# First slot of a fused attention and expert kernel: transposes into another PSUM pool, and a new order of the last routing, the tables and the splits

## The chip, the cores and the metric

The kernel runs on one core of a Trainium2 chip. The metric is device time in microseconds (us) of one launch. A time is the median of several runs; a profile is one further execution of its own, recorded by the hardware profiler.

## The reference

Three stages follow one another.

```python
# attention, 8 x 8 heads, 576 positions, width 64; softmax over the width for q, over the positions for k
kv = einsum('bhsd,bhse->bhde', softmax(k, 2), v);  x = einsum('bhsd,bhde->bhse', softmax(q, -1), kv)
# x as 4608 rows of 512; each row goes to one of 8 experts (512 -> 1024 -> 512)
logits = x @ w_gate + modality_bias[modality_id];  e = argmax(logits, 1);  gate = max(softmax(logits))
out[e == i] = gate * (relu(x[e == i] @ w1[i]) @ w2[i])
# a dense pair of layers, 512 -> 2048 -> 512, weights given as 64-bit floats
h = out @ w_in;  y = max(0.01 * h, h) @ w_out
```

## The kernel before

Every fp32 product of the expert and dense layers is made as three products of rounded parts: a matrix is split into a high part (a CAST on ACT) and a low part (source minus high part, on DVE). `split` (L506 and L507) does that for weights, `pass1` (L663, with L665 on ACT and the `low` of L666 on DVE) for the hidden values.

**Attention with routing (0 to 167 us).** Pairs of heads go through `phase_k`, `phase_q` and `phase_x`; rows of x leave in 36 chunks of 128 rows. A chunk is transposed (`tq`, L238), exponentiated on ACT (L240), multiplied (`xp`, L248 or L253), normalised on DVE (L260, L262: the evacuation) and stored. All of this work stands in one list of (time, function) entries, sorted by time; its unit is one chunk, and the time is only a place in the order in which instructions are written, since each engine runs its own in order. `route(c0, c1, ...)` adds the routing of chunks c0 to c1; entries at 36 and later are left over and are written by `tail(f)`, called after block f of the first slot.

**Expert slots (167 to about 588 us).** A slot is up to 512 rows of one expert. Slot 0 holds rows of the first half of the attention alone, so its gather can start early. For each slot: an index read (`idload`, L620, on SP), a cast of the indices on DVE (`xids`, L624), four indirect DMAs from POOL, one for each tile of 128 rows (`xgather`, L629, 1 MB in all into `xg`), four gates on ACT (`xgate`, L638), and four `xprep(k)`: four 128x128 transposes on PE into a PSUM tile `tp` (L649), a CAST on ACT (`xh`, L651) and a subtraction on DVE (`xl`, L652). The rows of a slot are laid out four apart, so that both ACT and DVE write with a stride of four elements. Then pass 1 (L663, eight blocks f of twelve matmuls) and pass 2 (L674, four blocks t of 24 matmuls, with a function `mid` called in the middle of each; the results are copied by ACT in L680). The next slot's rows are gated and transposed within pass 2 of the slot before: in slot 0 the gates in `mid` of t=1, two `xprep` each in `mid` of t=2 and t=3; in later slots the gates before pass 2 and the `xprep` in `mid` of t=1 and t=2.

Weights come in through a ring of five 512 KB staging tiles (`st_109` to `st_113`), loaded by SP in order (L597, eight items for each slot: four for w1, four for w2); `wsplit(s, which, c)` splits an item and then lets SP load up to four items ahead. A weight split therefore paces the loads.

**Conversions.** Beside slots 0 to 7 the 64-bit weights of the dense layers are turned into split fp32 by 16 conversions, each of them four steps, written by `step()`. A step is DVE work: step 0 is L721 and L722, step 1 is L726 and L727, step 2 is L729 and L730, and step 3 is four L734, an ACT CAST (`rh`, L506, 128x1792) and a DVE subtraction (`rl`, L507, 128x1792) that waits for the CAST. Step 0 also issues the stores of the conversion before and the loads of the next one (`w`, L705, two of 512 KB). Which step falls on which place of a slot follows from the count alone. `slot` calls `step` after blocks f = 1, 3, 5, 7 of pass 1, after t = 0, 1, 2 of pass 2 and in `mid` of t = 3, and once more at f = 6 for s > 3.

**Slot 0.** `slot0` and `slot0b` write out this order by hand. The routing of the last three chunks, the scatter of the row tables by POOL, the tables of the slots from 1 on (`slot_tables`, three pieces, ending in `ti`, L500 and L501), and the splits of slot 0's second weights all lie beside pass 1.

After the slots come the dense layers (L954, L968, then L1129 and L1151), from 618 us to the end; they are not touched.

Of the kernel before, what the change touches and what calls it, by code (L numbers as in the profile page):

```python
# [9 lines left out]
F32 = mybir.dt.float32  # L10
# [91 lines left out]
def attention(ctx, pools, tc, cst, a, region, xd, first):  # L102
# [10 lines left out]
    for i in range(4):  # L113
        t = one.tile([128, 4, 146], F32, name=f"kvx{i}")
# [279 lines left out]
    def route(c0, c1, times, ts, rate=0.0):  # L394


        fs, scats = phase_r(c0, c1)
        t = 0
        for n, (name, f) in enumerate(fs.items()):
            t = times.get(name, t)  # L400
            add(c1 + t, [(0.001 * n, f)])
        for n, (f, c) in enumerate(scats):
            if rate:
                at = c1 + ts + rate * n
                add(at, [(0.0, paced, min(int(at) - 1, NPAIR * NC - 1), f, c)])
            else:
                add(c1 + ts, [(0.001 * n, f, c)])
# [6 lines left out]
    route(9, 18, late9, 9.4, 0.5)  # L414
    route(18, 27, mid, 5.05, 0.5)
    route(27, 33, fast, 3.03)
    route(33, 36, dict(r0=0.2, rm=2.1), 2.3)
    add(1.0, [(0.1, cst["prep"])])
    add(0.0, first.steps())
    steps.sort(key=lambda x: x[:2])  # L420
# [120 lines left out]
def experts(pools, tc, cst, a, region, xd, dense, did, wops):  # L541
# [58 lines left out]
    AHEAD = NST - 1  # L600
    nload = [0]

    def loads_to(n):
        while nload[0] < min(n, len(items)):
            wload(*items[nload[0]])
            nload[0] += 1
# [37 lines left out]
    xlow = {}  # L644

    def xprep(k, wait=False):
        tp = ps2.tile([128, 4, 128], F32, tag="t", name="tp")
        for t in range(4):
            nc.tensor.transpose(out=tp[:, t], in_=xg[:, t, 128 * k:128 * k + 128], identity=ident)  # L649
        hi, lo = (x[:, k].rearrange("d (p t) -> d t p", t=4) for x in (xh, xl))  # L650
        nc.scalar.copy(out=hi, in_=tp)  # L651
        low = lambda: nc.vector.tensor_tensor(out=lo, in0=tp, in1=hi.bitcast(F32), op=ALU.subtract)  # L652
        if wait:
            xlow[k] = low
        else:
            low()
# [26 lines left out]
    def prepare():  # L683
        G = nc.gpsimd
        l = [(19.0 + 0.4 * n, loads_to, n + 1) for n in range(NST)]
        l += [(23.6, place1)] + [(23.65 + 0.7 * c, wsplit, 0, 1, c, G if c < 3 else None, 8) for c in range(4)]
        l += [(23.5, idload, 0), (25.1, xids, 0), (25.6, xgather, 0), (28.0, place2)]
        l += [(28.4 + 0.3 * t, xgate1, 0, t) for t in range(4)]
        for k in range(4):
            l += [(29.45 + k, xprep, k, True), (30.05 + k, lambda k=k: xlow.pop(k)())]  # L690
        return l + [(34.9, place3)]

    first.prepare = prepare
# [65 lines left out]
    def slot0(tail, sp):  # L759
        G, rows = nc.gpsimd, slice(0, SLOT)  # L760
        nc.sync.dma_start(out=did[0:SLOT].rearrange("(p t) c -> p (t c)", t=4), in_=idts[0].rearrange("p t c -> p (t c)"))
        tables = None
        lows = []
        for f in range(8):
            lows.append(pass1(f, rows))
            tail(f)
            if f == 1:
                lows.pop(0)()
                wsplit(0, 2, 0, None, 8)
                wsplit(0, 2, 1, None, 8)  # L770
                lows.pop(0)()
            elif f == 2:
                tables = slot_tables(tc, sp, ep, ps, cst, first, ti)
                next(tables)
            elif f == 3:
                lows.pop(0)()
                next(tables)
                lows.pop(0)()
                next(tables, None)
                idload(1)  # L780
                loads_to(11)
            elif f == 5:
                lows.pop(0)()
                wsplit(0, 2, 2, None, 8)
            elif f == 6:
                lows.pop(0)()
                wsplit(0, 2, 3, None, 8)
        for low in lows:
            low()

    def slot0b(step):
        rows = slice(0, SLOT)
        xload(1)
        loads_to(8 + AHEAD)
        idload(2)
        for t in range(4):
            def mid():
                if t == 0:
                    wsplit(1, 1, 0)
                elif t == 1:  # L800
                    xgate(1)
                else:
                    xprep(2 * t - 4)
                    xprep(2 * t - 3)
            pass2(t, 0, mid, rows)
            if t < 3:
                wsplit(1, 1, t + 1)
            step()

    def slot(s, step=lambda: None, mid2=lambda t: None, rows=slice(0, SLOT)):  # L810
        if s + 1 < NSLOT:
            xload(s + 1)
        for f in range(8):
            pass1(f, rows)()
            if f % 2 == 0:
                wsplit(s, 2, f // 2)
                if f == 6 and s > 3:
                    step()
            else:
                step()  # L820
# [23 lines left out]
    def rest(ctx, pre):  # L844
        wp = ctx.enter_context(tc.tile_pool(name="wp", bufs=1, reuse_waits="tile"))
        ys.extend(wp.tile([128, DM], F32, name=f"y{i}") for i in range(2))
        with ExitStack() as cctx:
            conv = conversions(cctx.enter_context(tc.tile_pool(name="cv", bufs=1, side="right", reuse_waits="tile")))
            next(conv)
            step = lambda: next(conv, None)  # L850
            slot0b(step)
            for s in range(1, NSTATIC - 1):
                slot(s, step=step)
            for _ in conv:
                pass
# [426 lines left out]
```

## Time and profile before

| | us |
|---|---|
| median of three runs (lowest, highest) | 1358.45 (1357.91, 1358.45) |
| the profiled execution's own time | 1359.47 |
| its span in the trace | 1357.7 |
| PE busy | 1297.9 (96% of the span) |
| DVE busy | 1035.6 (76%) |
| ACT busy | 584.3 (43%) |
| POOL busy | 348.0 (26%) |

The span runs from the first instruction to the last; the rest of the profiled time lies around it. PE is TensorE, DVE VectorE, ACT ScalarE, POOL GpSimd, and SP the engine that issues most DMAs. A busy time is the sum of the instructions' durations. Matmuls overlap in the pipeline: a row of the trace gives the start of a group and the duration of the whole group, and the distance of two starts is what a matmul costs. Idle time of an engine stands in square brackets with what ended it.

### The profile page before, as it was taken

To read this page: it belongs to the slowest core of one execution; us is meant where nothing else is said; L and a number is where in the kernel's file an instruction comes from. 1 tells how busy PE (TensorE), PEld (TensorE's weight loads), DVE (VectorE), ACT (ScalarE), POOL (GpSimd) and SP (SyncE) were. 2 spreads that over 40 slices of the span, in tenths; PEclk is the share of its full clock that TensorE was granted. 3 is DMA by queue.
4 is the path that set the end of the run, shared out by engine and by line. 5 is a ranking of instruction groups with operands and counts; after the bars stand their busy time and mean duration, and the time that the engine had idled before them with its cause. 6 is when DMAs were issued, how large, how long until landed. Compare 5 with 4: busy or idle time off the path is not lost.

```text
span 1357.7 us, 23466 instructions
## 1 busy us (share of the span) xinstructions
PE 1297.9 (96%) x9185; PEld 1214.5 (89%) x9185; DVE 1035.6 (76%) x1380; ACT 584.3 (43%) x914; POOL 348.0 (26%) x283
## 2 busy tenths in 40 slices
PE   6998699999999999998999999999969999999998
PEld 5988587888888877888999999999969999999998
DVE  5789766787778878557788888888757778778775
ACT  4556435554555555562333323333324334333432
POOL 2227841011101110112344343444411221121121
PEclk9999899999999999998999999999989999999999
DMA  9876347788879887978732333333894434344430
GB/s 370 350 288 194 124 123 248 256 260 274 289 246 311 290 274 226 310 222 312 291 125 111 139 128 152 125 145 118 335 372 125 148 125 140 125 132 140 125 117 32
DMA packets 146442, 279.04 MB, mean 206 GB/s; under 512 B 18192, under 2 KB 69904, under 8 KB 145424
## 3 DMA queue, kind: packets, MB, share of 16 engines
q1 hardware_dynamic: 121536, 207.93, 45.7%
q10 hardware_dynamic: 17232, 48.48, 9.0%
q0 software_dynamic: 7552, 21.02, 4.5%
q8 instruction: 75, 1.23, 0.4%
q14 instruction: 47, 0.39, 0.1%
HBM read 181.07 MB, written 96.32 MB: 204 GB/s over the span
## 4 chain that ended last, share of the span: by engine, by line
PE 23%; issue 23%; POOL 5%; DMA 2%; DVE 0%; POOLq 0%; SPq 0%; ACT 0%; DVEq 0%; ACTq 0%
PE hp L954 23%; POOL out L1151 4%; DMA wi<-wid 2%; DMA hd<-ht 1%; POOL s L999 0%; DVE ht L968 0%; SPq L924 0%; POOLq L1151 0%; POOL s L1000 0%; POOLq L1278 0%; DVE ht L1004 0%; DVE xt L939 0%; DVE xt L940 0%; DVE ht L1008 0%; ACT s L998 0%
## 5 line engine op out<-in xcount | busy, mean ns | idle before, releaser
L954 PE MATMUL hp<-xh,wi 128*128 128x256 f32 x1152 | 210.1, 280 | 0.8 <-DMA wi<-wid 0.8
L663 PE MATMUL hp<-xq,xk 128*128 128x512 f32 (+1 forms) x640 | 191.0, 382 | 4.5 <-DVE xr L262 3.5
L1129 PE MATMUL yp<-wi,x 128*128 128x256 f32 x1152 | 188.4, 280 | 0.8 <-DVE x L507 0.8
L954 PEld LDWEIGHTS hp<-xh,wi 128*128 128x128 f32 x1152 | 178.7, 188 | 1.2 <-ACT xh L506 1.0
L1129 PE MATMUL yp<-wi,wi 128*128 128x256 f32 x1200 | 174.7, 280 | 3.9 <-ACT wi L506 1.8
L954 PE MATMUL hp<-x,wi 128*128 128x256 f32 x1296 | 163.7, 285 | 3.7 <-ACTq L864 3.7
L1129 PEld LDWEIGHTS yp<-wi,wi 128*128 128x128 f32 x1200 | 160.0, 188 | 4.4 <-ACT wi L506 2.0
L954 PEld LDWEIGHTS hp<-x,wi 128*128 128x128 f32 x1296 | 160.3, 192 | 3.9 <-ACTq L864 3.9
L954 PE MATMUL hp<-xl,wi 128*128 128x256 f32 x576 | 161.4, 280 | 0.0
L1129 PEld LDWEIGHTS yp<-wi,x 128*128 128x128 f32 x1152 | 158.6, 189 | 1.0 <-DVE x L507 1.0
L629 POOL DMA_INDIRECT xg<-xd,idi x44 | 52.3, 1188 | 360.9 <-ACT xq L665 200.5
L663 PEld LDWEIGHTS hp<-xq,xk 128*128 128x128 f32 x640 | 119.1, 190 | 27.8 <-DVE xr L262 3.5
L674 PE MATMUL yp<-xq,xk 128*128 128x512 f32 (+1 forms) x400 | 142.4, 385 | 0.8 <-DVE xq L666 0.8
L507 DVE TENSOR_TENSOR xv<-st,xk 128x1024 fp32r<-128x1024 f32 x81 | 99.7, 1232 | 54.2 <-ACT xk L506 53.5
L1151 POOL DMA_INDIRECT out<-yo,idx x36 | 61.5, 1707 | 307.5 <-DVE idx L1145 289.0
L663 PE MATMUL hp<-xq,xv 128*128 128x512 f32 (+1 forms) x320 | 122.0, 381 | 0.0
L674 PE MATMUL yp<-xq,xv 128*128 128x512 f32 (+1 forms) x320 | 121.8, 381 | 0.0
L968 DVE SCALAR_TENSOR_TENSOR ht<-ht 128x1024 f32<-128x1024 f32 x72 | 113.3, 1583 | 1.8
L954 PEld LDWEIGHTS hp<-xl,wi 128*128 128x128 f32 x576 | 108.3, 188 | 0.0
L999 POOL TENSOR_TENSOR s<-s,s 128x512 f32<-128x512 f32 x36 | 49.4, 1373 | 190.9 <-DVE s L996 98.8
L506 ACT CAST xk<-st 128x1024 fp32r<-128x1024 f32 x84 | 87.5, 1044 | 13.3 <-ACT y L680 8.3
L665 ACT ACTIVATE xq<-hp 128x512 fp32r<-128x512 f32 (+1 forms) x80 | 46.1, 577 | 99.2 <-PE hp L663 82.0
(215 smaller groups left out, 2411.9 us busy)
## 6 DMA issues: line engine op xcount, KB each, us to landing
st<-in_w SPq DMA_DIRECT2D x88, 512.0 KB
hd<-ht ACTq DMA_DIRECT2D x72, 512.0 KB
xt<-hd SPq DMA_DIRECT2D x18, 1024.0 KB
hr<-hd SPq DMA_DIRECT2D x18, 1024.0 KB
wi<-wid SPq DMA_DIRECT2D x28, 512.0 KB
wi<-wod SPq DMA_DIRECT2D x6, 2048.0 KB
v<-in_v SPq DMA_DIRECT2D x16, 650.0 KB
k<-in_k SPq DMA_DIRECT2D x16, 576.0 KB
```

Of the source, the lines that this page charges most:

```text
L506: nc.scalar.copy(out=hi, in_=src)
L507: (eng or nc.vector).tensor_tensor(out=lo, in0=src, in1=hi.bitcast(F32), op=ALU.subtract)
L629: nc.gpsimd.indirect_dma_start(out=xg[:, t], out_offset=None, in_=xd[0:n], in_offset=bass.IndirectOffsetOnAxis(ap=idis[s % 2][:, t:t + 1], ...
L663: nc.tensor.matmul(hp[:, rows], lhsT=w[:, k, 128 * f:128 * f + 128], rhs=x[:, k, rows], start=(n == 0), stop=(n == 11))
L665: nc.scalar.activation(out=hh[:, f, rows], in_=hp[:, rows], func=AF.Relu)
L674: nc.tensor.matmul(yp[:, rows], lhsT=w[:, f, 128 * d:128 * d + 128], rhs=h[:, rows], start=(n == 0), stop=(n == 23))
L954: self.nc.tensor.matmul(bank[:, g], lhsT=w[:, h, k, 128 * g:128 * g + 128], rhs=x[:, k], start=(n == 0), stop=(n == 5))
L968: V.scalar_tensor_tensor(out=c, in0=c, scalar=0.01, in1=c, op0=ALU.mult, op1=ALU.max)
L999: G.tensor_tensor(out=s[6], in0=s[6], in1=s[5], op=ALU.add)
L1129: nc.tensor.matmul(bank, lhsT=x[:, k], rhs=w[i][:, h, k], start=(c == 0), stop=(c == 23))
L1151: ins = nc.gpsimd.indirect_dma_start(out=out, out_offset=bass.IndirectOffsetOnAxis(ap=idi[s % 2][:, t:t + 1], axis=0), in_=y[:, t], in_off ...
```

## The change

Three parts:

1. `xprep` with `wait=True` (slot 0 alone) takes its PSUM tile from the pool `ps` ("kv") instead of `ps2` ("t"), and PE writes the four transposes interleaved, so that the CAST and the subtraction read and write 512 consecutive elements. The gates and the `xprep` of slot 0 stand 0.2 and 0.25 earlier in the list.
2. The last routing's entries and its scatters move from 36 + 2.1 and 2.3 to 36 + 1.2 and 1.3, which is from `tail(2)` to `tail(1)`. In `slot0` the pieces of the tables stand beside blocks 1 to 3, the splits of the second weights beside blocks 4 to 7, and the loads run less far ahead.
3. In `slot0b` the first conversion's loads are written after t = 0 (they were written ahead of the slot) and only three steps follow (there were four); slot 3 gets the extra step at f = 6.

```diff
--- before.py
+++ after.py
@@ -414,7 +414,7 @@
     route(9, 18, late9, 9.4, 0.5)
     route(18, 27, mid, 5.05, 0.5)
     route(27, 33, fast, 3.03)
-    route(33, 36, dict(r0=0.2, rm=2.1), 2.3)
+    route(33, 36, dict(r0=0.2, rm=1.2), 1.3)
     add(1.0, [(0.1, cst["prep"])])
     add(0.0, first.steps())
     steps.sort(key=lambda x: x[:2])
@@ -644,10 +644,16 @@
     xlow = {}
 
     def xprep(k, wait=False):
-        tp = ps2.tile([128, 4, 128], F32, tag="t", name="tp")
+        hi, lo = (x[:, k].rearrange("d (p t) -> d t p", t=4) for x in (xh, xl))
+        if wait:
+            tp = ps.tile([128, 128, 4], F32, tag="kv", name="tp").rearrange("d p t -> d t p")
+            flat = lambda x: x.rearrange("d t p -> d p t")
+        else:
+            tp = ps2.tile([128, 4, 128], F32, tag="t", name="tp")
+            flat = lambda x: x
         for t in range(4):
             nc.tensor.transpose(out=tp[:, t], in_=xg[:, t, 128 * k:128 * k + 128], identity=ident)
-        hi, lo = (x[:, k].rearrange("d (p t) -> d t p", t=4) for x in (xh, xl))
+        hi, lo, tp = flat(hi), flat(lo), flat(tp)
         nc.scalar.copy(out=hi, in_=tp)
         low = lambda: nc.vector.tensor_tensor(out=lo, in0=tp, in1=hi.bitcast(F32), op=ALU.subtract)
         if wait:
@@ -685,9 +691,9 @@
         l = [(19.0 + 0.4 * n, loads_to, n + 1) for n in range(NST)]
         l += [(23.6, place1)] + [(23.65 + 0.7 * c, wsplit, 0, 1, c, G if c < 3 else None, 8) for c in range(4)]
         l += [(23.5, idload, 0), (25.1, xids, 0), (25.6, xgather, 0), (28.0, place2)]
-        l += [(28.4 + 0.3 * t, xgate1, 0, t) for t in range(4)]
+        l += [(28.2 + 0.3 * t, xgate1, 0, t) for t in range(4)]
         for k in range(4):
-            l += [(29.45 + k, xprep, k, True), (30.05 + k, lambda k=k: xlow.pop(k)())]
+            l += [(29.2 + k, xprep, k, True), (29.8 + k, lambda k=k: xlow.pop(k)())]
         return l + [(34.9, place3)]
 
     first.prepare = prepare
@@ -759,39 +765,26 @@
     def slot0(tail, sp):
         G, rows = nc.gpsimd, slice(0, SLOT)
         nc.sync.dma_start(out=did[0:SLOT].rearrange("(p t) c -> p (t c)", t=4), in_=idts[0].rearrange("p t c -> p (t c)"))
-        tables = None
         lows = []
         for f in range(8):
             lows.append(pass1(f, rows))
             tail(f)
+            if f:
+                lows.pop(0)()
             if f == 1:
-                lows.pop(0)()
-                wsplit(0, 2, 0, None, 8)
-                wsplit(0, 2, 1, None, 8)
-                lows.pop(0)()
-            elif f == 2:
                 tables = slot_tables(tc, sp, ep, ps, cst, first, ti)
+            if f in (1, 2, 3):
                 next(tables)
-            elif f == 3:
-                lows.pop(0)()
-                next(tables)
-                lows.pop(0)()
-                next(tables, None)
+            if f == 3:
                 idload(1)
-                loads_to(11)
-            elif f == 5:
-                lows.pop(0)()
-                wsplit(0, 2, 2, None, 8)
-            elif f == 6:
-                lows.pop(0)()
-                wsplit(0, 2, 3, None, 8)
-        for low in lows:
-            low()
-
-    def slot0b(step):
+                loads_to(9)
+            if f > 3:
+                wsplit(0, 2, f - 4)
+        lows.pop(0)()
+
+    def slot0b(start, step):
         rows = slice(0, SLOT)
         xload(1)
-        loads_to(8 + AHEAD)
         idload(2)
         for t in range(4):
             def mid():
@@ -802,10 +795,15 @@
                 else:
                     xprep(2 * t - 4)
                     xprep(2 * t - 3)
+                if t == 3:
+                    step()
             pass2(t, 0, mid, rows)
             if t < 3:
                 wsplit(1, 1, t + 1)
-            step()
+            if t == 0:
+                start()
+            elif t > 1:
+                step()
 
     def slot(s, step=lambda: None, mid2=lambda t: None, rows=slice(0, SLOT)):
         if s + 1 < NSLOT:
@@ -814,7 +812,7 @@
             pass1(f, rows)()
             if f % 2 == 0:
                 wsplit(s, 2, f // 2)
-                if f == 6 and s > 3:
+                if f == 6 and s > 2:
                     step()
             else:
                 step()
@@ -846,9 +844,8 @@
         ys.extend(wp.tile([128, DM], F32, name=f"y{i}") for i in range(2))
         with ExitStack() as cctx:
             conv = conversions(cctx.enter_context(tc.tile_pool(name="cv", bufs=1, side="right", reuse_waits="tile")))
-            next(conv)
             step = lambda: next(conv, None)
-            slot0b(step)
+            slot0b(step, step)
             for s in range(1, NSTATIC - 1):
                 slot(s, step=step)
             for _ in conv:
```

On PE, at the end of the attention, the transposes of slot 0's rows (`tp`) and the matmuls of the chunks (`xp`) change places. Before:

```order
L649 MATMUL tp<-cf,xg 128x128 x4
L238 MATMUL tq<-cf,q_1105 128x128 x4
L248 MATMUL xp<-kvx_145,eq 128x146 x4
L649 MATMUL tp<-cf,xg 128x128 x4
L238 MATMUL tq<-cf,q_1105 128x128 x4
L248 MATMUL xp<-kvx_145,eq 128x146 x4
```

After, with L655 for L649:

```order
L238 MATMUL tq<-cf,q_1105 128x128 x4
L655 MATMUL tp<-cf,xg 128x128 x4
L248 MATMUL xp<-kvx_145,eq 128x146 x4
L238 MATMUL tq<-cf,q_1105 128x128 x4
L655 MATMUL tp<-cf,xg 128x128 x4
L248 MATMUL xp<-kvx_145,eq 128x146 x4
```

A group of transposes now stands between a `tq` and the `xp` of the chunk ahead.

On DVE, at the end of slot 0's pass 1 (`xv<-hp` and `xq<-hp` are the lows of blocks, `xv<-st` a split, `idi` the index cast ahead of slot 1's gather). Before:

```order
L666 SCALAR_TENSOR_TENSOR xv<-hp,xq 128x512
L507 TENSOR_TENSOR xv<-st_110,xk 128x1024
L666 SCALAR_TENSOR_TENSOR xv<-hp,xq 128x512
L507 TENSOR_TENSOR xv<-st_111,xk 128x1024
L666 SCALAR_TENSOR_TENSOR xq<-hp,xq 128x512 x2
L624 CAST idi_118<-idt_115 128x4
L507 TENSOR_TENSOR xv<-st_112,xk 128x4x256
```

After, with L672 for L666:

```order
L672 SCALAR_TENSOR_TENSOR xk<-hp,xq 128x512
L507 TENSOR_TENSOR xv<-st_113,xk 128x1024
L672 SCALAR_TENSOR_TENSOR xv<-hp,xq 128x512
L507 TENSOR_TENSOR xv<-st_109,xk 128x1024
L672 SCALAR_TENSOR_TENSOR xv<-hp,xq 128x512
L507 TENSOR_TENSOR xv<-st_110,xk 128x1024
L672 SCALAR_TENSOR_TENSOR xq<-hp,xq 128x512
L507 TENSOR_TENSOR xv<-st_111,xk 128x1024
L672 SCALAR_TENSOR_TENSOR xq<-hp,xq 128x512
L624 CAST idi_118<-idt_115 128x4
L507 TENSOR_TENSOR xv<-st_112,xk 128x4x256
```

The last split of the second weights now stands between the low of block 6 and that of block 7, and the index cast behind both.

On DVE, in pass 2 of slot 1 (`xv<-st` are the splits of slot 2's first weights, L652 or L658 the subtractions of the first two `xprep`). Before:

```order
L734 TENSOR_TENSOR r<-r 128x256 x4
L507 TENSOR_TENSOR rl<-r,rh 128x1792
L507 TENSOR_TENSOR xv<-st_110,xk 128x4x256
L507 TENSOR_TENSOR xv<-st_111,xk 128x4x256
L721 TENSOR_SCALAR r<-w 128x1024
L722 TENSOR_SCALAR r<-r 128x1024
L652 TENSOR_TENSOR xq<-tp,xq 128x4x128 x2
```

After, with L740 for L734, L735 and L736 for L729 and L730:

```order
L735 TENSOR_TENSOR r<-r,w 128x1024
L736 SCALAR_TENSOR_TENSOR r<-w,r 128x1024
L507 TENSOR_TENSOR xv<-st_110,xk 128x4x256
L507 TENSOR_TENSOR xv<-st_111,xk 128x4x256
L740 TENSOR_TENSOR r<-r 128x256 x4
L507 TENSOR_TENSOR rl<-r,rh 128x1792
L658 TENSOR_TENSOR xq<-tp,xq 128x4x128 x2
```

Step 3 of a conversion (L734 or L740, then `rl`) now stands between the splits and the subtractions, where step 0 stood.

## Rows read from the trace of the kernel before

**Rows 1.** Waits of PE, 120 to 235 us: total, times, longest (us).

```profile
PE tp L649 <- ACT xg L638: 2.5, 3, 1.3
```

**Rows 2.** PE timeline, starts of passes: start, duration, instruction, count.

```profile
167.24 1.22 PE L663 MATMUL hp<-xq,xk 128*128 128x512 f32 x2 [3.45 <-DVE xr L262]
...
191.99 0.39 PE L674 MATMUL yp<-xq,xk 128*128 128x512 f32 x1
...
220.29 0.39 PE L663 MATMUL hp<-xq,xk 128*128 128x512 f32 x1
...
242.05 0.39 PE L674 MATMUL yp<-xq,xk 128*128 128x512 f32 x1
...
265.63 0.39 PE L663 MATMUL hp<-xq,xk 128*128 128x512 f32 x1
...
469.90 0.39 PE L674 MATMUL yp<-xq,xk 128*128 128x512 f32 x1
...
494.87 0.39 PE L663 MATMUL hp<-xq,xk 128*128 128x512 f32 x1
...
516.63 0.39 PE L674 MATMUL yp<-xq,xk 128*128 128x512 f32 x1
...
541.80 0.39 PE L663 MATMUL hp<-xq,xk 128*128 128x512 f32 x1
```

**Rows 3.** ACT and DVE timelines around slot 0's row transposes.

```profile
155.29 1.08 ACT L651 CAST xq<-tp 128x512 fp32r<-128x512 f32 x1 [0.17 <-issue]
165.79 0.27 ACT L255 ACTIVATE ri<-xp,eps 128x8 f32<-128x8 f32 x1 [5.05 <-remote]
...
156.92 1.11 DVE L652 TENSOR_TENSOR xq<-tp,xq 128x512 fp32r<-128x512 f32 x1
160.40 0.69 DVE L262 TENSOR_TENSOR xr<-xp,ri 128x512 f32<-128x512 f32 x1 [0.20 <-DVE ri L260]
```

**Rows 4.** Windows of core 0: us, busy by engine, PEclk, DMA share, GB/s.

```profile
163.00:168.00 5.00, 1.55 (x8) 0.95 (x7) 1.51 (x4) 0.77 (x5) 2.44 (x5) 0.50 0.01 0
172.00:173.00 1.00, 1.00 (x5) 0.73 (x5) 0.00 (x0) 0.23 (x1) 0.69 (x2) 0.74 0.03 1
...
...
211.00:212.00 1.00, 1.00 (x4) 0.81 (x3) 1.00 (x1) 1.00 (x2) 0.00 (x0) 0.50 0.83 315
```

**Rows 5.** Timelines of ACT, DVE, POOL and PE: slot 1's gather.

```profile
192.19 0.60 ACT L665 ACTIVATE xq<-hp 128x512 fp32r<-128x512 f32 x1 [1.19 <-PE hp L663]
193.53 1.05 ACT L506 CAST xk<-st 128x1024 fp32r<-128x1024 f32 x1 [0.75 <-DMA st<-in_w]
...
207.59 1.36 ACT L638 ACTIVATE xg<-xg,idt 128x512 f32<-128x512 f32 x2 [0.48 <-DMA xg<-xd,idi]
...
193.50 0.16 DVE L624 CAST idi<-idt 128x4 int32<-128x4 f32 x1
...
198.41 1.00 POOL L629 DMA_INDIRECT xg<-xd,idi  x1 [0.32 <-issue]
...
205.59 0.27 PE L649 MATMUL tp<-cf,xg 128*128 128x128 f32 x1
```

**Rows 6.** DMA from 190 to 207 us: packets; queue, kind: packets, MB, share.

```profile
DMA packets 3719, 5.28 MB, mean 310 GB/s; under 512 B 384, under 2 KB 2432, under 8 KB 3717
...
q1 hardware_dynamic: 3257, 3.95, 72.9%
```

**Rows 7.** Slot 8's gather: last issue; its queue in 504 to 506 us.

```profile
501.75 1.00 POOL L629 DMA_INDIRECT xg<-xd,idi  x1 [0.30 <-issue]
...
q0 software_dynamic: 131, 0.41, 55.1%
```

**Rows 8.** DVE and PE timelines, pass 2 of slot 6.

```profile
477.63 1.23 DVE L507 TENSOR_TENSOR xv<-st,xk 128x1024 fp32r<-128x1024 f32 x1 [1.11 <-ACT xk L506]
...
484.02 2.11 DVE L652 TENSOR_TENSOR xq<-tp,xq 128x512 fp32r<-128x512 f32 x2
...
485.16 0.66 PE L649 MATMUL tp<-cf,xg 128*128 128x128 f32 x4 [0.59 <-DVE xq L652]
```

## The prediction

> **What bounds the kernel now.** I read the shares by engine first: PE is busy for 1297.9 of 1357.7 us, so a gain must come from a place where PE waits, or from the order that decides who waits. The list of PE's waits then shows how few there are around the change, and the one that the change touches with certainty: the transposes of slot 1's rows wait three times, 2.5 us in all, for the gates on ACT [rows 1]. The PE timeline, read at the starts of the passes, turns waits into time. From slot 0's pass 1 to the dense layers PE goes from pass to pass without a pause, so what pass 1 of slot 0 starts later, or a pass takes longer, arrives at the end in full. Pass 2 takes 28.30 us in slot 0 (191.99 to 220.29), 23.58 in slot 1, 24.97 in slot 6 and 25.17 in slot 7 [rows 2]. It is the same work each time (96 matmuls and 16 transposes), so 23.58 is what it takes undisturbed, and slot 0 loses 4.72, slot 6 loses 1.39, slot 7 loses 1.59. Third, the timelines of ACT, DVE and POOL at these places tell what was late.
>
> **The sum has three terms:** A, when pass 1 of slot 0 starts; B, slot 0's pass 2; C, pass 2 of slots 1 to 3. From slot 4 on both kernels write the same steps at the same places, since the conversion step that slot0b gives up is made up at f = 6 of slot 3 (28 steps are behind when slot 4 begins, before and after).
>
> **A: the transposes of slot 0's rows.** Each of the four `xprep` has a CAST of 1.08 us on ACT and a subtraction of 1.11 on DVE, which write at a stride of four [rows 3]. Flat ops of the same size are in the trace: 0.60 for an ACT op of 128x512 out of PSUM [rows 5] and 0.69 for a DVE op of 128x512 [rows 3]. So 0.48 on ACT and 0.42 on DVE go, four times. What counts is the chain that ends in pass 1: the subtraction at 156.92, the routing's DVE ops behind it, the evacuation at 160.40, and the last chunk's matmuls. Three of the four subtractions lie in this DVE chain close enough to its end to move it: 3 x 0.42 = 1.3 us sooner. The casts lie on ACT beside DVE's other ops, and I count them as nothing (1.9 at most, if each were on the path). Behind the last chunk, however, the trace shows something that no duration explains: ACT sits idle for 5.05 us until 165.79 with the releaser given as remote, and PE waits 3.45 us for DVE's evacuation after that, until 167.24 [rows 2, 3]. I assume that this comes again as it is, and merely sooner. The last entries of the list, the gates and transposes 0.2 to 0.25 sooner, exchange a group of four transposes with one of four `xp`; both have to be done, and I count that as nothing. Bounds for A: −7.8 below (the wait of 5.05 goes; PE's clock is at 0.50 from 163 to 168 and at 0.74 in 172:173 [rows 4], so some 5.3 us of pass 1 run at half speed, of which half, 2.7, would come back too; that makes 7.8, in which I let the 1.3 vanish); +4.0 above (5.3 less the 1.3), if the interleaved writes of the transposes cost, which no row shows: a transpose takes some 0.165 us of a group of four (0.66, [rows 8]), and 16 of them at three times that would add 5.3. [...]
>
> [...] No run here shows a strided write into PSUM by PE. [...] The stride itself does cost on the other side of the copy, as 1.08 against 0.60 shows.
>
> **Also moved, at nothing.** The last routing and its scatters lie a block sooner and the tables beside blocks 1 to 3; the tables' DVE ops are the same ones, and PE's pass 1 needs none of them. The splits of the second weights now come at blocks 4 to 7, each one CAST of 1.05 [rows 5] and one DVE op of 1.23 [rows 8]; with a low, a DVE op of 0.69 like the evacuation [rows 3], that is 1.9 us in a block of 2.72 (21.76 / 8), so DVE keeps pace, and the last split is done at about 195.1, while pass 2 needs its columns only behind three quarters of its first block, at 192.0 + 0.75 x 5.5 = 196.1. That cover is 1.0 us thin; if it fails, PE waits, and I put at most 1 us on it.
>
> **B: slot 1's gather.** Before, the index cast stands at 193.50, the last of four gathers is issued until 199.41, and its rows have landed for the last two gates at 207.59, 8.2 us later; PE comes to the transposes at 205.59 [rows 5]. The gap costs the 2.5 us of [rows 1], and the clock then falls to 0.50 (211:212, [rows 4]); together 4.72. After, the order on DVE puts the last split and the low of block 7 ahead of the cast. By before's clock: the block-7 activation on ACT starts at 192.19 and takes 0.60, the CAST of the split 1.05 [rows 5], the split 1.23 [rows 8], the low 0.69 [rows 3]: the index cast comes at 192.19 + 0.60 + 1.05 + 1.23 + 0.69 = 195.8, which is 2.3 us later, and the last issue ends at 201.7. So the gather is issued later. Against that stands what it shares the DMA engines with. Before, from 190 to 207, SP's queue moves 3.95 MB beside the gather, and the engines move 5.28 MB in all, 310 GB/s [rows 6]. After, SP's loads follow the splits one by one: from 195.1 on (the end of the split that frees the buffer) a staging tile, a second one behind the next split, and the two loads of the conversion, 2.0 MB; then the gather's 1.0 and 0.3 of results. 3.3 MB at 310 GB/s take 10.6 us: until 205.7, if the gather is the last of these. The other end of the trace is slot 8, whose last issue ends at 502.75 and whose gather's packets are over by 506, at most 3.3 us later [rows 7]: that would be 205.0 here. To cost PE nothing the last rows must have landed by about 205 (PE's last four transposes stand at 205.9, and one or two gates of 0.68 lie between). I take 205.7: a rest of 0.7 us in the wait, and another 0.5 for columns at half clock, B = −4.7 + 1.2 = −3.5. Bounds: −4.7 (no wait is left) and +2.3 (as late behind its issue as before).
>
> **C: the conversion's phase.** Slot0b runs three steps in place of four, so in slots 1 and 2 each place holds the step ahead of the one it held: f = 1, 3, 5, 7 get steps 3, 0, 1, 2, and t = 0, 1, 2 get 3, 0, 1 (before: 0, 1, 2, 3 and 0, 1, 2). The order on DVE shows it: step 3 now stands between the splits and the first two `xprep`'s subtractions. This is what slot 6 of the kernel before has: behind the split at 477.63 (where DVE had been idle for 1.11, so that nothing of the steps ahead still counts) come step 3's four ops, its wait for ACT's CAST, and the long subtraction; the `xprep` subtractions start only at 484.02, and PE's next transposes wait at 485.16, since their banks are not free [rows 8]. Pass 2 of slot 6 loses 1.39, and the same order in slots 1 and 2 should lose the same. Slot 3 gets the step at f = 6 and with it exactly slot 7's sequence (3, 0, 1, 2, 3, then 0), and should lose slot 7's 1.59 [rows 2]. C = 1.39 + 1.39 + 1.59 = +4.4. Bounds: 0, if DVE gets to the splits of slots 1 to 3 early enough to be ahead of PE; +5.5 (half a microsecond more in two of them), if a wait lets the clock fall as in slot 0 once.
>
> **Sum:** −1.3 − 3.5 + 4.4 = −0.4 us against the profiled execution's 1359.47, its 1357.7 of span and 1.8 around it. The runs shown have a median 1.0 below that, so I forecast 1358.45 − 0.4 = 1358.05. A difference within 0.2% (2.7 us) is what a measurement of this kernel can't tell from none.
>
> **Rivals.**
> - *The idle 5 us before pass 1 go* (16 in 100). For it: no instruction fills them, and the PE order around them changes. Against: the chain into them, tq, xp, evacuation, is the same. A = −7.8 in place of −1.3: 1351.5.
> - *The phase costs nothing in slots 1 to 3* (16 in 100). For it: slots 1 to 3 run at 23.58 with a step 3 at f = 7, so DVE has slack there. Against: the wait of slot 6 starts from a point where DVE was idle. C = 0: 1353.6.
> - *The gather stays as late behind its issue as before* (14 in 100), and the change is slower. The mechanism is the wait of slot 1's transposes: rows 8.2 us behind an issue that is 2.3 later land at 209.9 by before's clock. For it: the engines may be as full with 2 MB as with 4, as long as something is there at each moment. Against: slot 8, with 3.3. B = +2.3: 1358.45 − 1.3 + 2.3 + 4.4 = 1363.9. It decides from a landing at about 206 on, where B is −3.1 and the sum passes zero. [...]
> - *Interleaved transposes are slow* (6 in 100): at three times the duration A = +4.0, and the sum 1363.4; at half of that increase 1360.7.
>
> **Chances.** The forecast has 48 in 100, with a range of its own from 1355.5 (A −1.7, B −4.7, C +3.5) to 1361 (A 0, B −2, C +4.6). Faster by more than 0.2% are the first two rivals, 32; slower the last two, 20; the rest is within it. The range from 1351.3 to 1361.8 leaves out the third rival and the worse half of the fourth, and takes in the first at its edge.
>
> **What would show it.** A: the first L663 row at about 165.9 with CAST and subtraction at 0.6 and 0.7; interleaving is harmless if a group of four transposes still takes 0.66. B: slot 0's pass 2 at 24 to 26 us, the index cast about 3.6 us behind its start, and a wait of PE for ACT's gates under 1 us. C: pass 2 of slots 1 and 2 at 25.0 and of slot 3 at 25.2, each with waits of the transposes for DVE's `xq`, and slots 4 to 8 unchanged. The forecast is wrong if slots 1 to 3 stay at 23.6, if ACT's idle 5 us are gone, or if slot 0's pass 2 stays at 28.

## The result, and the profile after

The changed kernel takes 1365.67 us (median of five runs, 1365.20 to 1370.36) against 1358.20 of the kernel before, measured beside it; the ratio is 1.0062, with a 95% interval from 1.0047 to 1.0077. It is slower, by 7.5 us where −0.4 was forecast, and outside the range. The profiled execution has a span of 1363.4 us, 5.7 above that of before.

The starts of PE's passes in the changed kernel (L669 is pass 1, L680 pass 2; columns: start, duration, instruction, idle time before it) answer to [rows 2]:

```profile
162.39 0.73 PE L669 MATMUL hp<-xq,xk 128*128 128x512 f32 x2 [0.46 <-DVE xr L262]
...
170.28 1.22 PE L669 MATMUL hp<-xq,xk 128*128 128x512 f32 x2 [4.87 <-DVE xr L262]
...
192.07 0.39 PE L680 MATMUL yp<-xq,xk 128*128 128x512 f32 x1
...
222.83 0.39 PE L669 MATMUL hp<-xq,xk 128*128 128x512 f32 x1
...
244.59 0.39 PE L680 MATMUL yp<-xq,xk 128*128 128x512 f32 x1
...
269.54 0.39 PE L669 MATMUL hp<-xq,xk 128*128 128x512 f32 x1
...
337.98 0.39 PE L680 MATMUL yp<-xq,xk 128*128 128x512 f32 x1
...
363.17 0.39 PE L669 MATMUL hp<-xq,xk 128*128 128x512 f32 x1
```

Pass 1 of slot 0 starts 4.85 us sooner and ends where it ended, 0.08 us later, since it stops behind its first block. Pass 2 takes 30.76 us in slot 0 (28.30 before), 24.95 in slot 1, 24.91 in slot 2 and 25.19 in slot 3 (23.58, 23.57, 23.57 before). In the prediction's terms, with A taken at the end of pass 1, that is A = +0.08, B = +2.46, C = +4.33, together 6.87. Slots 4 to 8 give 0.3 back and the rest of the span, from the last start of pass 2 on, 0.8; that rest, the same instructions in all kernels, varies between 755.9 and 759.1 us over the 14 profiles of this study.

Two of PE's waits from 120 to 235 us (total, times, longest), to [rows 1]:

```profile
PE hp L669 <- DVE xr L262: 5.3, 2, 4.9
PE tp L655 <- ACT xg L638: 3.6, 4, 1.4
```

Around the start of pass 1, on ACT, DVE, PE and POOL, to [rows 3]:

```profile
154.06 0.58 ACT L657 CAST xq<-tp 128x512 fp32r<-128x512 f32 x1
...
168.83 0.27 ACT L255 ACTIVATE ri<-xp,eps 128x8 f32<-128x8 f32 x1 [7.38 <-remote]
...
155.04 0.68 DVE L658 TENSOR_TENSOR xq<-tp,xq 128x512 fp32r<-128x512 f32 x1
...
153.30 0.60 PE L655 MATMUL tp<-cf,xg 128*128 128x128 f32 x4
...
159.96 1.74 PE L253 MATMUL xp<-kvx,eq 128*64 128x146 f32 x16 [1.85 <-issue]
...
166.59 0.98 POOL L363 DMA_INDIRECT region<-tg,ix  x1 [0.16 <-issue]
```

The copies have the sizes that were forecast, 0.58 and 0.68, and a group of four interleaved transposes takes 0.60 at a granted clock of 1.00 (153.3 to 153.9). Then ACT sits idle for 7.38 us, longer than before, for a result that PE finished at 161.7 (the end of its last `xp`), and the evacuation behind it frees the bank that block 1 needs. PE loses more than its 4.87 us of waiting: from 170.28 to 175 us the granted clock is 0.50, with the starts of two matmuls 0.43 us apart, and pass 1 takes 29.68 us, against 22.30 in e1 below, where they are 0.23 apart from the first block on. The POOL line is the last of a row of indirect DMAs (the scatters of the routing) that POOL issues one behind the other.

Slot 1's gather, on ACT, DVE and POOL, to [rows 5]:

```profile
192.27 0.60 ACT L671 ACTIVATE xq<-hp 128x512 fp32r<-128x512 f32 x1 [1.10 <-PE hp L669]
192.76 1.99 ACT L506 CAST xk<-st 128x1024 fp32r<-128x1024 f32 x2
...
209.80 0.72 ACT L638 ACTIVATE xg<-xg,idt 128x512 f32<-128x512 f32 x1 [0.23 <-DMA xg<-xd,idi]
...
195.58 0.16 DVE L624 CAST idi<-idt 128x4 int32<-128x4 f32 x1
...
200.72 1.19 POOL L629 DMA_INDIRECT xg<-xd,idi  x1 [0.30 <-issue]
```

The index cast stands at 195.58 (195.8 was worked out), and the last issue ends at 201.91 (201.7 was worked out). The last gate that waits for rows starts 7.9 us behind it (8.2 before).

What the DMA engines carried meanwhile: first SP's issues, then the bytes from 195.1 us, where the prediction begins to count, to 209.25, where the gather's last packet ends (q1 is SP's queue, q0 the gather's):

```profile
188.25 5.17 SPq L597 DMA_DIRECT2D st<-in_w  x4
...
195.09 2.18 SPq L597 DMA_DIRECT2D st<-in_w  x2
197.32 0.97 SPq L711 DMA_DIRECT2D w<-in_win  x2
201.06 0.39 SPq L597 DMA_DIRECT2D st<-in_w  x1
...
DMA packets 2526, 4.47 MB, mean 316 GB/s; under 512 B 321, under 2 KB 901, under 8 KB 2524
...
q1 hardware_dynamic: 2061, 3.14, 67.5%
q0 software_dynamic: 319, 1.05, 20.1%
```

The rate is the one that was assumed, 316 for 310 GB/s; the bytes are not, 4.47 MB for 3.3. Of the four loads that SP issued from 188.25 on (2.1 MB) only 1.5 MB had moved by 195.1, and a third weight load follows at 201.06.

Pass 2 of slot 1, on DVE and PE, and PE's waits from 222 to 364 us, to [rows 8]:

```profile
252.33 1.23 DVE L507 TENSOR_TENSOR xv<-st,xk 128x1024 fp32r<-128x1024 f32 x1 [2.29 <-ACT xk L506]
253.47 1.55 DVE L740 TENSOR_TENSOR r<-r 128x256 f32<-128x256 f32 x4
...
258.73 2.09 DVE L658 TENSOR_TENSOR xq<-tp,xq 128x512 fp32r<-128x512 f32 x2
...
259.86 0.66 PE L655 MATMUL tp<-cf,xg 128*128 128x128 f32 x4 [0.60 <-DVE xq L658]
...
PE tp L655 <- DVE xq L658: 2.5, 6, 0.6
```

This is slot 6 of before again: split, step 3, the subtractions 6.4 us behind the split's start, and PE waiting 0.60 where it waited 0.59. Six such waits stand in slots 1 to 3, where before had none.

### The profile page after: what moved, and what is told of

It is laid out like the page before. It is cut to its first block, busy times and chain, and to the rows that moved or that the text cites. A ratio compares the mean times of both kernels' runs of the same rounds, so it can differ in the third digit from the quotient of the medians.

```text
span 1363.4 us, 23468 instructions
## 1 busy us (share of the span) xinstructions
PE 1300.5 (95%) x9185; PEld 1215.7 (89%) x9185; DVE 1034.4 (76%) x1380; ACT 582.4 (43%) x914; POOL 346.9 (25%) x283
## 4 chain that ended last, share of the span: by engine, by line
PE 26%; issue 23%; POOL 5%; POOLq 0%; ACT 0%
PE hp L951 26%; POOL out L1148 4%; POOL s L996 0%; POOLq L1148 0%; POOL s L997 0%; POOLq L1275 0%; ACT xh L506 0%; ACT s L995 0%; POOL ht L977 0%; POOLq L977 0%
## 5 line engine op out<-in xcount | busy, mean ns | idle before, releaser
L669 PE MATMUL hp<-xq,xk 128*128 128x512 f32 (+1 forms) x640 | 191.1, 382 | 6.1 <-DVE xr L262 5.3
L669 PEld LDWEIGHTS hp<-xq,xk 128*128 128x128 f32 x640 | 118.9, 190 | 29.7 <-DVE xr L262 5.8
L680 PE MATMUL yp<-xq,xk 128*128 128x512 f32 (+1 forms) x400 | 142.8, 386 | 0.8 <-DVE xq L672 0.8
L680 PE MATMUL yp<-xq,xv 128*128 128x512 f32 (+1 forms) x320 | 122.0, 381 | 0.0
L669 PE MATMUL hp<-xq,xv 128*128 128x512 f32 (+1 forms) x320 | 121.8, 381 | 0.0
L680 PEld LDWEIGHTS yp<-xq,xk 128*128 128x128 f32 x400 | 75.5, 190 | 14.9 <-DVE xq L672 1.2
```

The source lines that it names most:

```text
L669: nc.tensor.matmul(hp[:, rows], lhsT=w[:, k, 128 * f:128 * f + 128], rhs=x[:, k, rows], start=(n == 0), stop=(n == 11))
L680: nc.tensor.matmul(yp[:, rows], lhsT=w[:, f, 128 * d:128 * d + 128], rhs=h[:, rows], start=(n == 0), stop=(n == 23))
```

## The experiments

Three theories had to be told apart. First, the conversion steps' new places cost 4.3 us by themselves; the rival was that slots 1 to 3 are late only because slot 0 is. Second, the rows of a gather come a fixed time behind the last issue, against the view of the prediction, in which the bytes beside them decide. Third, the long idle time of ACT in front of pass 1 (called the hold from here on) belongs to something other than the chain of copies; its candidate, POOL's row of indirect DMAs, came up only with the profiles of the first two groups.

Each group of four ran on one chip beside the kernel before: 1351.29 us in the first group, 1359.32 in the second, 1358.81 in the third. Ratios are to these; "gather lag" is, for slot 1, from the end of POOL's last issue to the start of the last gate that waited for rows, all in us from the profiles.

| kernel | ratio (interval) | pass 2 starts | slot 0 | slots 1, 2, 3 | gather lag |
|---|---|---|---|---|---|
| before, as profiled first | | 191.99 | 28.30 | 23.58, 23.57, 23.57 | 8.2 |
| changed | 1.0062 (1.0047 to 1.0077) | 192.07 | 30.76 | 24.95, 24.91, 25.19 | 7.9 |
| e1, steps at old places | 1.0010 (0.9997 to 1.0024) | 184.69 | 29.48 | 23.57, 23.67, 23.54 | 6.2 |
| e2, early gather | 1.0014 (1.0004 to 1.0024) | 184.45 | 24.42 | 24.97, 24.95, 25.15 | 6.9 |
| e3, both | 0.9979 (0.9964 to 0.9993) | 185.07 | 23.58 | 23.57, 23.69, 23.57 | 6.0 |
| e4, part 1 alone | 0.9989 (0.9976 to 1.0002) | 184.14 | 25.89 | 23.57, 23.57, 23.58 | 8.0 |
| f1, before | 0.9989 (0.9975 to 1.0004) | 189.85 | 30.43 | 23.57, 23.57, 23.58 | 8.0 |
| f2, changed | 1.0043 (1.0029 to 1.0057) | 191.56 | 30.49 | 24.96, 24.93, 25.19 | 7.4 |
| f3, late load | 1.0027 (1.0016 to 1.0038) | 192.51 | 28.52 | 24.98, 24.94, 25.17 | 6.6 |
| f4, part 1, early gather | 0.9958 (0.9945 to 0.9972) | 192.15 | 24.63 | 23.58, 23.57, 23.57 | 8.3 |
| g1, before, paced | 1.0040 (1.0024 to 1.0056) | 194.56 | 32.39 | 23.55, 23.54, 23.55 | 8.0 |
| g2, changed, paced | 1.0068 (1.0046 to 1.0090) | 196.56 | 29.93 | 24.94, 24.97, 25.14 | 8.0 |
| g3, e3 paced | 0.9994 (0.9983 to 1.0005) | 195.87 | 23.57 | 23.57, 23.69, 23.57 | no wait |
| g4, e3 again | 0.9976 (0.9963 to 0.9989) | 191.78 | 23.96 | 23.58, 23.66, 23.55 | 7.2 |

**e1: the conversion steps at their old places**

```diff
-            elif t > 1:
+            else:
                 step()
...
-                if f == 6 and s > 2:
+                if f == 6 and s > 3:
```

> The changed kernel with four conversion steps in slot 0 again and the extra step from slot 4 on, so that the steps fall on the places in slots 1 to 3 that they had before. If the step's place is what makes pass 2 of slots 1 to 3 longer (24.95, 24.91 and 25.19 us in the changed kernel), they go back to 23.6 and the time falls by 4.3 us, to about 1361.4. If they are longer because slot 0 runs late and everything behind it is pushed, they stay at 25 and the time stays near 1365.7.

Slots 1 to 3 are back at 23.6 us although slot 0 takes 29.48, so the steps' places cost 4.3 us and slot 0's lateness nothing. What was not expected: this kernel has the changed kernel's instructions up to pass 2 of slot 0, but pass 1 takes 22.30 us here and 29.68 there. ACT, PE and POOL of e1 at this place:

```profile
162.19 0.27 ACT L255 ACTIVATE ri<-xp,eps 128x8 f32<-128x8 f32 x1 [2.65 <-PE xp L253]
...
160.41 1.74 PE L253 MATMUL xp<-kvx,eq 128*64 128x146 f32 x16 [1.84 <-DVE w L320]
...
167.06 0.98 POOL L363 DMA_INDIRECT region<-tg,ix  x1 [0.16 <-issue]
```

ACT goes on at 162.19, 0.04 us behind the end of PE's last `xp`, while POOL's row of indirect DMAs is still running. The trace's record of PE's semaphore says the same: in the changed kernel it counts only at 168.81, for an `xp` that ended at 161.70. So it is PE's signal that is late there, and not some other wait. The hold is not in the program's order, then: on this chip it is missing in all four kernels that were profiled. It is the likely reason why the times there, that of the kernel before included, are 6 to 8 us lower; the kernel before was not profiled on this chip. The absolute time expected was therefore of no use; the comparison with before, +1.1 us, stands.

**e2: the gather at block 5**

```diff
+            if f == 5:
+                xload(1)
             if f > 3:
                 wsplit(0, 2, f - 4)
...
-        xload(1)
         idload(2)
```

> The changed kernel with the index cast and slot 1's gather written at block 5 of pass 1, ahead of the splits of blocks 5 to 7. If the rows land a fixed 8 us behind the last issue, the last issue ends near 196.4 instead of 201.9, the rows are there near 204.4, PE waits for no gate, and pass 2 of slot 0 takes 23.6 to 24.3 us instead of 30.8: about 1359. If the landing is set by what else the DMA engines carry, it moves by less than the issue, the rows come at 206 or later, and pass 2 stays above 26 us: 1361 or more.

ACT and PE of e2, the last gate and PE's wait from 184 to 210 us:

```profile
198.39 0.72 ACT L638 ACTIVATE xg<-xg,idt 128x512 f32<-128x512 f32 x1 [2.21 <-DMA xg<-xd,idi]
...
PE tp L655 <- ACT xg L638: 0.3, 1, 0.3
```

The cast moved to 184.16 (it waited 4.27 us for the index read), 0.3 us ahead of pass 2 in place of 3.5 behind its start, and the last gate started 6.9 us behind the last issue. Pass 2 of slot 0 takes 24.42 us, just above the 24.3 that was expected: the wait for the gather is worth 5.1 (against e1) to 6.3 us (against the changed kernel), and an earlier issue takes it away.

**e3 and g4: both edits**

> Both edits, the old places of the conversion steps and the early gather. If the two losses are separate they add: slots 0 to 3 near 23.6 to 24.3 us each in pass 2, 11 us below the changed kernel, about 1354.5, which is faster than the kernel before. If one loss hides the other, it is no better than the better of the two alone, 1359 or more.

> The changed kernel with the old places of the conversion steps and the early gather, again, beside the others. On the earlier chip it was 3.0 us below the kernel before. If the two repairs hold on any chip, it is 3 to 5 us below the kernel before here as well.

The losses add: e3 lies 4.1 us below e1 and 4.8 below e2. The repaired kernel beats the kernel before by 3.0 us on one chip and by 4.5 on another (medians; both intervals lie below 1). Pass 2 of slots 0 to 3 is at 23.6 to 24.0.

e2 and e3 also bear on the second theory. They differ in the steps' places alone, but with step 0 go the loads and stores of a conversion. The bytes by queue for slot 3's gather, from the end of its last issue to the end of its last packet, 3.8 us in e2 (first two lines) and 7.1 in e3:

```profile
q1 hardware_dynamic: 530, 0.53, 40.4%
q0 software_dynamic: 160, 0.52, 36.8%
...
q1 hardware_dynamic: 1066, 1.50, 65.0%
q0 software_dynamic: 319, 1.05, 37.8%
```

For slots 2 and 4 it is 4.8 and 3.4 us in e2 and 6.8 and 6.8 in e3. So the rows do not come a fixed time behind the last issue: the same gather is later where more bytes of SP go beside it.

**e4: part 1 alone** (the new `xprep` in the kernel before, nothing moved)

> The kernel before with only the first part of the change: the interleaved transposes in the other PSUM pool, nothing moved. If the shorter casts and subtractions count as forecast, pass 1 ends 1.3 us sooner than the 191.99 of before, about 1357. If the late release of ACT in front of pass 1 (the wait marked remote) sets the start, pass 1 ends within 0.3 us of 191.99 whatever the copies take. If interleaved transposes are slow, a group of four takes well over 0.66 us.

On this chip, without the hold, e4 is 1.75 us below the kernel before by the medians, with an interval that includes no change, so −1.3 is neither shown nor excluded; pass 2 starts at 184.14, the earliest of the group. The interleaved transposes are not slow: a group of four takes 0.65 us, as before (0.66 in [rows 8]). No profile of the kernel before exists on this chip. Beside e1 it shows what the other parts cost slot 0: the index cast stands 1.5 us behind the start of pass 2 here and 3.5 in e1, and pass 2 takes 25.89 us against 29.48.

**f1 and f2: before and changed, on one chip**

> The kernel before, unchanged, for its profile beside that of the changed kernel on one chip. If the late release of ACT in front of pass 1 comes from the chip or the execution, this profile and the next both have it or both lack it, and without it pass 1 of slot 0 takes 22.3 us from a start near 162.5 instead of 24.75 from 167.24. If it comes from this kernel's order, it is here again, with pass 1 starting near 167.

> The changed kernel, unchanged, on the same chip. The place of the conversion steps accounts for +4.3 us over the kernel before wherever it runs; the gather for +2 to +3 if it lands a fixed time behind its issue; the shorter copies for -1.3 to 0. So 5 to 6.5 us above the kernel before. If the whole of the 7.5 us first measured belongs to the kernel, it is 7.5 here as well; if part of it was the late release falling differently in the two, it is less.

Both show the hold. ACT and POOL in f1, the kernel before; the last line is POOL's in the first profile of before:

```profile
168.81 0.27 ACT L255 ACTIVATE ri<-xp,eps 128x8 f32<-128x8 f32 x1 [4.61 <-remote]
...
166.39 0.98 POOL L363 DMA_INDIRECT region<-tg,ix  x1 [0.16 <-issue]
...
163.62 0.98 POOL L363 DMA_INDIRECT region<-tg,ix  x1 [0.16 <-issue]
```

ACT is released 1.4 us after POOL's row of indirect DMAs ends (167.37). It was 1.2 in the first profile of before (POOL's row ended at 164.60 there), 1.3 in that of the changed kernel (167.57), 1.5 in f2, 1.2 in f3, 1.4 in g4 and only 0.6 in f4 (168.40 for a row that ended at 167.83). The release follows the row, not the kernel. f2 lies 5.8 us above the kernel before of its group, as expected. In this pair A is +1.71, B +0.06 and C +4.36: C repeats to 0.03 us, while A and B depend on where the hold and the gather fall in one execution. Nor are A and B independent: f1 starts pass 2 of slot 0 2.14 us sooner than the first profile of before (189.85 for 191.99) and ends it at the same time (220.28 for 220.29), since it then waits longer for the gather. Their sum is steadier, +2.54 in the first pair and +1.77 in this one.

**f3: the conversion's loads one block later**

```diff
-            if t == 0:
+            if t == 1:
                 start()
```

> The changed kernel with the first conversion's two loads (1 MB) issued after t = 1 of slot 0's pass 2, behind the split that frees the next staging tile, instead of after t = 0: the gather has 1 MB less beside it, its own issue stays where it was. If the landing is set by what the DMA engines carry, the last rows come 2 to 3 us sooner and pass 2 of slot 0 is shorter by as much than in the changed kernel of this call. If the rows come some 7 us behind their issue whatever is loaded, the pass stays within 0.5 us of it.

```profile
201.14 1.20 POOL L629 DMA_INDIRECT xg<-xd,idi  x1 [0.30 <-issue]
...
208.93 0.72 ACT L638 ACTIVATE xg<-xg,idt 128x512 f32<-128x512 f32 x1 [1.53 <-DMA xg<-xd,idi]
```

These are POOL's last issue and the last gate. The edit did less than was meant, as SP's issues show:

```profile
195.53 6.34 SPq L597 DMA_DIRECT2D st<-in_w  x3
201.92 1.00 SPq L711 DMA_DIRECT2D w<-in_win  x2
```

The conversion's loads leave at 201.92 (197.12 in f2), still 6 us ahead of the gather's last packet at 208.13, and a weight load has moved ahead of them. From the first issue to the last packet the other queues moved 2.62 MB, against 2.96 in f2: 0.3 MB less, not 1. The gather lag is 0.8 us shorter, but its issue ended 0.8 later, so the last gate stands where it stood (208.93 for 208.88). Pass 2 is 2.0 us shorter, of which 0.95 is its own later start. With one profile of each, this run decides nothing between the two theories.

**f4: part 1 and an early gather, no other part** (`xload(1)` at block 6 of the kernel before, ahead of the last split)

> The kernel before with the first part of the change (interleaved transposes) and slot 1's gather written at block 6, ahead of the last split: neither the moved routing and tables nor the moved conversion steps. If the second part of the change is worth nothing by itself, this does as well as the changed kernel with both repairs, 3 us below the kernel before, with pass 2 of slot 0 under 24.5 us. If the sooner tables are what makes an early gather possible, the index read comes too late here, pass 2 of slot 0 stays at 25 us or more, and the time is within 1.5 us of the kernel before.

Pass 2 of slot 0 takes 24.63 us, between the two bounds, and the kernel is 4.7 us below the kernel before, the best ratio of the study. The sooner tables of the second part are not needed for an early gather, though some 1 us of the wait is left.

**g1, g2 and g3: pauses in POOL's row**

```diff
-    route(18, 27, mid, 5.05, 0.5)
-    route(27, 33, fast, 3.03)
+    route(18, 27, mid, 6.55, 0.5)
+    route(27, 33, fast, 4.6)
```

(and the last routing's scatters at 1.7 in g2 and g3, so that POOL's order stays.)

> The kernel before with the scatters of the third routing paced 1.5 chunks later (and those of the fourth behind them), so that POOL's row of indirect DMAs at 153 to 168 us has pauses while the last chunks run; the same scatters in the same order. In five of the profiles taken so far PE's signals arrive only 1.2 to 1.5 us after the last of that row has ended, whenever that is. If POOL's row holds them back, pass 1 of slot 0 starts near 163 and takes 22 to 23 us on a chip that shows the hold, and the time falls by 3 to 7 us. If the hold has another cause, ACT's idle time in front of pass 1 ends where it did, and later scatters gain nothing or cost up to 2 us. On a chip without the hold (pass 1 of 22.3 us in the unchanged order) the edit changes little either way.

> The changed kernel with the same pacing. If the hold goes in both, the difference to the kernel before with this pacing is the change without that disturbance: -0.5 to -1.3 us for the start of pass 2, 0 to 2.5 for the gather, +4.3 for the conversion steps, so 3 to 6 us slower than it.

> The changed kernel with the conversion steps at their old places and the early gather, and this pacing. If the hold is POOL's, it gains the same 3 to 7 us over the same kernel without the pacing (the next run) on a chip that shows the hold, and is the fastest of all. If the later scatters delay the index read instead, the gather comes later by as much and pass 2 of slot 0 grows above 24.5 us.

POOL and ACT in g1:

```profile
157.47 0.98 POOL L363 DMA_INDIRECT region<-tg,ix  x1 [0.64 <-issue]
160.99 0.18 POOL L375 COPY pace<-ri 1x1 f32<-1x1 f32 x1 [2.54 <-DVE ri L260]
161.74 0.98 POOL L363 DMA_INDIRECT region<-tg,ix  x1 [0.57 <-issue]
...
178.72 0.97 POOL L363 DMA_INDIRECT region<-tg,ix  x1 [0.31 <-issue]
...
164.72 0.27 ACT L255 ACTIVATE ri<-xp,eps 128x8 f32<-128x8 f32 x1 [3.70 <-PE xp L253]
...
181.05 0.60 ACT L665 ACTIVATE xq<-hp 128x512 fp32r<-128x512 f32 x1 [11.13 <-remote]
```

The end of the hold moved with the row, and the gain did not come. With a pause at 158.5 to 161.7 ACT has its result at 164.72 (168.81 in f1), and pass 1 starts at 164.80. But the row now runs without a pause from 161.74 to 179.69, and a hold stands inside pass 1: ACT idles for 11.13 us, until 1.4 us behind the row's new end, and pass 1 takes 29.76 us. In g2 and g3 it takes 33.07 and 32.62, with ACT released 2.0 and 0.7 us behind the row's end. Not all that PE releases comes late beside the row, nor does all of it wait for the row's end: in g1 ACT went on at 164.72, 3 us into the row and 0.04 behind the end of PE's `xp`, and in g2 at 172.80, in the midst of the row, for a matmul that had ended at 166.50. All in all the kernels with the pauses take 3.5 to 5.9 us more than those without (medians of g3 to g4, g1 to before). So g3, expected to be the fastest, is 3.5 us slower than g4; and since the hold went in neither g1 nor g2, their difference of 2.9 us does not give the change without it.

## Why the prediction was wrong

- **C was right**, in mechanism and size: +4.4 forecast, +4.33, +4.36 measured, and e1 takes it away. The rows of slots 6 and 7 of before were a full model of slots 1 to 3 after.
- **B failed**, and with it the sign: −3.5 forecast, +2.46 measured. The step that failed is the count of the bytes ahead of the last row: "2.0 MB; then the gather's 1.0 and 0.3 of results. 3.3 MB at 310 GB/s take 10.6 us: until 205.7, if the gather is the last of these." The rate held, at 316 GB/s, and so did the last condition, since the engines run empty behind the gather (a DMA share of 0.09 from 210 to 212 us). But 4.47 MB went through from 195.1 on, until 209.25: SP's queue carried 3.14 MB where 2.0 were counted, because the prediction began with an empty queue and left out a third weight load. The step before it, the later issue, was right: the cast 2.1 us later (2.3 forecast), the end of the last issue 2.5. Slot 8's 3.3 us was no bound for slot 1 either: 0.4 MB moved beside the gather there. The third rival, "as late behind its issue as before", has about the right price, +2.3, and the gather lag was indeed nearly the same (7.9 for 8.2). That is a coincidence: slot 3's gather, the same in both, ends 3.8 us behind its issue in e2 and 7.1 in e3. In the second pair B was +0.06, because f1's pass 2 started sooner and waited longer; the prediction summed A and B as if they were independent.
- **A failed**: "I assume that this comes again as it is, and merely sooner". The copies became as short as forecast and pass 1 began 4.85 us sooner, but the hold ended 1.3 us behind POOL's row of indirect DMAs, as it had ended 1.2 behind it before, and that row went on to 167.57 (164.60 before), so it came back behind the first block. So the 1.3 us were not to be had: +0.08 and +1.71. The rival in which the hold goes was no property of the change either: it was missing on one chip, in all four kernels profiled there.
- **That interleaved transposes cost nothing** was the author's estimate, and the −1.3 contains it: no row of the kernel before has a strided write into PSUM by PE. The runs bear it out: at a granted clock of 1.00 four interleaved transposes take 0.60 us in the changed kernel, and four contiguous ones 0.66 in [rows 8].
- The thin cover of the last split held: no wait of PE for it in pass 2 of slot 0.

What stays open is why PE's signals come late beside POOL's row on some chips and not on another, and what part 1 brings without the hold, since e4's interval includes no change. That the row causes the hold is argued and not shown: it rests on ten profiles in which the release follows the row's end by 0.6 to 2.0 us, and on g1, where that end was moved by 12 us and the release with it; leaving the row out was not tried. That the bytes set the landing in slot 1 rests on the count above and on slots 2 to 4 of e2 and e3; no run took more than 0.3 MB from beside slot 1's gather.

## What to carry to other kernels

When a change drops or adds one step of work that is dealt out by a count, every later place gets another step: look for a stretch of the old trace that already has the new pattern, and read the price there. Price an indirect gather by the bytes that go through beside it (slot 3's ended 3.8 us behind its issue beside 0.53 MB of SP's queue and 7.1 beside 1.50), and begin the count with what was issued earlier and has not yet moved, here 4.5 MB in place of 3.3. Take the lag of a sibling in the trace as a price only if the same loads lie beside it: slot 8's 3.3 us did not hold for slot 1, with 7.9. Moving slot 1's index cast ahead, by 3.8 us in e2, took most of the wait away (PE waits 0.3 us for the gates, 3.6 in the changed kernel). Two gains that end at the same wait need not add: f1 began pass 2 of slot 0 2.14 us sooner than the first profile of before and ended it at the same time, waiting longer for the gates (3.6 us, 2.5 there). An idle time that no instruction explains must not be carried along in a sum: find what it ends with, here, within 0.6 to 2.0 us, another engine's row of DMAs, before pricing a change in front of it.

## What the runs showed of the hardware

- In the ten profiles of the first pair, f1 to f4 and g1 to g4, ACT idled 4.6 to 11.1 us beside POOL's row of indirect DMAs for matmuls that had ended, and went on 0.6 to 2.0 us after the row ended; in the changed kernel PE's semaphore counted at 168.81 for an `xp` that ended at 161.70. In the four profiles of e1 to e4, all on one chip, the hold was missing beside the same row; ACT went on 0.04 us behind the end of PE's `xp` in e1.
- The last packet of a 1 MB gather in four indirect DMAs ended 3.2 to 8.2 us behind the end of the last issue in slots 1 to 10 of the kernel before, and 3.4 to 7.4 in those of the changed kernel; with the places of other loads changed, slot 3's went from 7.1 us in e3 to 3.8 in e2.
- Taking the stride out of a 128x512 copy's write made it 0.58 in place of 1.08 us on ACT and 0.68 in place of 1.11 on DVE. With PE writing PSUM at that stride instead, four transposes took 0.60 us at a granted clock of 1.00, and 0.65 to 0.66 without it.
